# Reordering the opening of a fused attention and feed-forward kernel: pieces of W_v and three copies out of PSUM

## The chip, the cores and the metric

The kernel runs on one core of a Trainium2 chip. Its time is the device time of one execution in microseconds (us); the median of several executions is compared. The engines are TensorE (PE in the profile), VectorE (DVE), ScalarE (ACT), GpSimd (POOL) and SyncE (SP). Each works through its own queue in program order, and semaphores order them among each other. SP issues nearly all DMAs here.

## The reference

One transformer block on x, 2048 rows of width 640, in bf16: attention with a linear kernel, then a gated feed-forward network, each on a layer-normed input and with a residual.

```
h  = x + A(layernorm(x));   result = h + B(layernorm(h))
A: q, k, v = split(x @ wqkv)                      # 32 heads of width 20
   pq, pk = q @ w_phi, k @ w_phi                  # per head
   phi = concat(softmax(p), softmax(-p))          # for q and for k
   kv = phi_k^T v;  z = sum(phi_k)                # over the rows
   o = (phi_q kv) / (phi_q z + 1e-6);  A = o @ wo
B: (gelu(x @ w_gate) * (x @ w_up)) @ w_down       # hidden width 1536
```

## The kernel before

**Tiles.** The 2048 rows are 16 tiles of 128 rows, four tiles to a block. The width of 640 is five chunks of 128 (`NC = 5`). A weight lies in SBUF with its rows split into these five chunks, so "row chunk c" of W_v is what the c-th product of a sum over the width needs. A product of v (`pv`) for one tile is ten matmuls: five row chunks for each of two halves of 320 columns.

**Stages.** The opening computes v for the first four tiles, "folds" w_phi into W_k (`fold`, L231 to 258, five folds, one for each chunk), and begins k. Then a loop over the 16 tiles computes k, its exponentials (`E`), their normalisation (`sk`, `rs`, `E`) and the sums over the rows (`kvp`). After that come q, the attention's output and the feed-forward network, which are nearly all matmuls.

**From x to v.** A tile of x is loaded, VectorE takes its statistics (`bn_stats` twice and an aggregate, L120 and L124), rstd is computed, and the tile is normalised (`ln`, L155 on VectorE, L150 on ScalarE). Tiles 0 to 3 are then transposed on TensorE into PSUM and copied back to SBUF (`transpose_to`, L163 and L164), on ScalarE for tiles 0 and 1 and on VectorE for tiles 2 and 3. From tile 4 on a transposing DMA does this (L166). For tiles 2 and 3 rstd is two small ScalarE operations (L130 and L131), for tile 3 put in the queue by hand between the copies of v of tiles 0 and 1 (`root[0]()`). From tile 4 on rstd is two GpSimd operations (L138 and L139). The result of v is copied out of PSUM by ScalarE (`v_ev`, L315).

**What sets the order.** The order of the opening is written out by hand, and every engine's queue follows it. `v_part(t, *cs)` issues the matmuls of tile t for the row chunks named. `ln_st(t, between=f)` puts f between the two `bn_stats` of the tile. The copy of fold d is on ScalarE when d is in `KA` and on VectorE otherwise. A pool of four two-bank PSUM tiles (`psG0`) serves transposes, v, folds and k: a matmul that starts a new tile waits until the copy out of the tile that lay there before is done. On SP's queue lie, in this order, the loads of x tiles 0, 1 and 2, two loads of W_v, x tile 3, the third load of W_v, x tiles 4 and 5, five transposing loads of W_k, x tiles 6 and 7 (L469); and then, in turn, the transposing DMA of each normalised tile and further loads of x. A queue that waits for a tile to be normalised holds what stands behind it.

Of the kernel before, what the change touches and what calls it, by code (L numbers as in the profile page):

```python
# [17 lines left out]
def kernel(  # L18
# [12 lines left out]
    nc = tc.nc  # L31
    P = 128
    S = 2048
    D = 640
# [10 lines left out]
    H0 = [(P * c) // Dh for c in range(NC)]  # L45
    NH = [(P * c + P - 1) // Dh - H0[c] + 1 for c in range(NC)]
    VP = (0, 2, 4, 6, 7, 9, 11, 12)
    KA, QA = (0, 1, 4), (0, 1, 2, 3, 4)
    LQ = (7, 9, 9, 9, 10)
    FQ = (10, 11, 12, 13, 14)  # L50

# [22 lines left out]
    w_v = A_wqkv.rearrange("(c p) n -> p c n", p=P)  # L74
# [9 lines left out]
    x_sb = [const.tile([P, 4, D], BF16, name=f"x_sb{b}") for b in range(NB)]  # L84
# [22 lines left out]
    def small(pool, shape, name, bufs=3):  # L107
        return pool.tile(shape, F32, name=name, bufs=bufs)

    def gtile(name):  # L110
        return psG.tile([P, 2, 512], F32, name=name, tag="G")

    def ln_stats(pool, tiles, tag, act=True, between=None, log=False):

        n = len(tiles)
        mv = small(pool, [P, n, nc.vector.BN_AGGR_DIM], "mv" + tag)
        stats = small(pool, [P, n, 2, nc.vector.BN_STATS_DIM], "stats" + tag)
        for j, xt in enumerate(tiles):
            for i in range(2):
                nc.vector.bn_stats(stats[:, j, i, :], xt[:, i * HD:(i + 1) * HD])  # L120
                if between and i == j == 0:
                    between()
        for j in range(n):
            nc.vector.bn_aggr(mv[:, j, :], stats[:, j])  # L124
        ve = small(pool, [P, n], "ve" + tag)
        rstd = small(pool, [P, n], "rstd" + tag)
        if log is not False:

            def root():
                nc.scalar.activation(ve, mv[:, :, 1], ACTF.Ln, bias=eps)  # L130
                nc.scalar.activation(rstd, ve, ACTF.Exp, scale=-0.5)  # L131

            if log is True:
                root()
            else:
                log.append(root)
        else:
            nc.gpsimd.tensor_scalar_add(ve, mv[:, :, 1], EPS)  # L138
            nc.gpsimd.tensor_tensor(rstd, ve, nhalf[:, 0:n], op=ALU.pow)  # L139

        mr = small(pool, [P, n], "mr" + tag)
        if act:
            for j in range(n):
                nc.gpsimd.tensor_scalar(mr[:, j:j + 1], mv[:, j, 0:1], rstd[:, j:j + 1], -1.0,
                                        op0=ALU.mult, op1=ALU.mult)
        return [(xt, mv[:, j, 0:1], rstd[:, j:j + 1], mr[:, j:j + 1]) for j, xt in enumerate(tiles)]
# [11 lines left out]
    def transpose_to(dst, src, on_pe, on_dve=False):  # L158

        if on_pe:  # L160
            tp = psG.tile([P, 16, P], BF16, name="tp", tag="G")
            for c in range(NC):
                nc.tensor.transpose(tp[:, c, :], src[:, c * P:(c + 1) * P], ident)  # L163
            (nc.vector.tensor_copy if on_dve else nc.scalar.copy)(dst, tp[:, 0:NC, :])  # L164
        else:
            nc.sync.dma_start_transpose(dst, src)  # L166
# [7 lines left out]
    p1 = p1_cm.__enter__()  # L174
    Wv = p1.tile([P, NC, D], BF16, name="Wv")
# [14 lines left out]
    nc.scalar.dma_start(wphi, phi_v.rearrange("(c p) f -> p c f", p=P))  # L190
    nc.scalar.add_instruction(mybir.InstLoadActFuncSet(name=nc.get_next_instruction_name(), act_func_set_id=6))
    nc.sync.dma_start(x_sb[0][:, 2:3, :], x_v[:, 2:3, :])
    nc.sync.dma_start(Wv[:, 0:2, :], w_v[:, 0:2, 2 * D:3 * D])
    nc.sync.dma_start(Wv[:, 2:4, :], w_v[:, 2:4, 2 * D:3 * D])
    nc.sync.dma_start(x_sb[0][:, 3:4, :], x_v[:, 3:4, :])
    nc.sync.dma_start(Wv[:, 4:5, :], w_v[:, 4:5, 2 * D:3 * D])
    nc.sync.dma_start(x_sb[1][:, 0:2, :], x_v[:, 4:6, :])

    def load_T(WT, i, *ds):
# [25 lines left out]
    def warm(*cols):  # L225
        for n in cols:
            nc.tensor.matmul(wu[:, 0, 0:n], lhsT=ones[:, 0:P], rhs=ones[:, 0:n], start=True, stop=True)
# [3 lines left out]
    def fold(WT, W2, quarters, ds=range(NC)):  # L231


        n, w = (2, QF) if quarters else (1, HD)
        runs = []
        for c in range(NC):
            lo, hi = H0[c] * Dh, (H0[c] + NH[c]) * Dh
            for r in range(2 * n):
                a, b = max(lo, r * w), min(hi, (r + 1) * w)
                if a < b:  # L240
                    runs.append((r // n, r, c, a, b))
        runs.sort()
        for d in ds:
            wa = gtile("wa")
            wr = wa.rearrange("p u (q x) -> p (u q) x", q=n)
            for i, (u, r, c, a, b) in enumerate(runs):
                nc.tensor.matmul(wr[:, r, a - r * w:b - r * w], lhsT=WT[:, c, d * P:(d + 1) * P],  # L247
                                 rhs=BD[:, c].rearrange("p a b -> p (a b)")[:, a - H0[c] * Dh:b - H0[c] * Dh],
                                 start=(i == 0 or runs[i - 1][0] != u),
                                 stop=(i + 1 == len(runs) or runs[i + 1][0] != u), skip_group_check=True)  # L250
            dst, src = W2[:, d, :].rearrange("p (u f) -> p u f", u=2), wr[:, :, 0:w]
            if quarters:
                dst = W2[:, d, :].rearrange("p (c r f) -> p r c f", c=NC, r=4)
                src = src.rearrange("p r (c f) -> p r c f", c=NC)
            if d in (QA if quarters else KA):
                nc.scalar.copy(dst, src)
            else:
                nc.vector.tensor_copy(dst, src)
# [6 lines left out]
    def ln_0(t):  # L265
        xt, mean, rstd, mr = lnp[t] = ln_stats(p1, [x_sb[0][:, t, :]], f"c{t}", False, None, True)[0]
        nc.gpsimd.tensor_scalar(nrstd[t], rstd, -1.0, None, op0=ALU.mult)
        if t == 0:
            nc.gpsimd.tensor_scalar(mr, mean, nrstd[0], None, op0=ALU.mult)
        xc = fp.tile([P, D], BF16, name="xc", bufs=2)  # L270
        nc.vector.tensor_scalar(xc, xt, mean, None, op0=ALU.subtract)
        return xc

    def ln_st(*tiles, act=True, between=None, log=False):
        for t, v in zip(tiles, ln_stats(p1, [x_sb[t // 4][:, t % 4, :] for t in tiles], "1", act, between, log)):
            lnp[t] = v

    def ln_ap(t, on_act=False, on_pe=False):
        ln = (ln_act if on_act else ln_dve)(p1, "1", *lnp[t])
        if on_pe:  # L280
            lnp[t] = ln
        else:
            transpose_to(LN1T[t // 4][:, :, t % 4 * P:(t % 4 + 1) * P], ln, False)

    def ln_tp(t, on_dve=False):
        transpose_to(LN1T[t // 4][:, :, t % 4 * P:(t % 4 + 1) * P], lnp[t], True, on_dve)

    def lnT(t, c):
        b, tl = divmod(t, 4)
        return LN1T[b][:, c, tl * P:(tl + 1) * P]  # L290
# [14 lines left out]
    def v_part(t, *cs):  # L305

        if 0 in cs:
            pv[t] = gtile("pv")
        for c in cs:
            for u in range(2):  # L310
                nc.tensor.matmul(pv[t][:, u, 0:HD], lhsT=lnT(t, c), rhs=Wv[:, c, u * HD:(u + 1) * HD],
                                 start=(c == 0), stop=(c == NC - 1))

    def v_ev(t):
        nc.scalar.activation(vS[t % NV][:, :, 1:VC].rearrange("p (u h) f -> p u h f", u=2),  # L315
                             pv[t][:, :, 0:HD].rearrange("p u (h f) -> p u h f", f=Dh), ACTF.Copy,
                             scale=lnp[t][2] if t in CT else 1.0)
# [123 lines left out]
    tr_c(0)  # L441
    tr_c(1)
    ln_st(2, act=False, log=True)
    bd(0, NC)
    st_act(1, 1)
    warm(*[P] * 4)
    v_part(0, 0, 1)
    v_part(1, 0, 1)
    ln_ap(2, on_pe=True)
    v_part(0, 2, 3)  # L450
    root = []
    ln_st(3, act=False, between=lambda: ln_tp(2, True), log=root)
    v_part(0, 4)
    v_ev(0)
    v_part(1, 2, 3)
    root[0]()
    v_part(1, 4)
    v_ev(1)
    v_part(2, *range(NC))
    d = ident.rearrange("p (r j) -> p r j", r=4)  # L460
# [2 lines left out]
    for s, j in ((0, VC + 1), (1, 0)):  # L463
        nc.gpsimd.tensor_scalar(sc[:, s:s + 1], row[:, 0, j:j + 1], -1.0, 1.0, op0=ALU.mult, op1=ALU.add)
        nc.gpsimd.tensor_scalar(bi[:, s:s + 1], row[:, 0, VC:VC + 1], 0.5e-6, row[:, 0, j:j + 1],
                                op0=ALU.mult, op1=ALU.add)
    ln_st(4, act=False, between=lambda: ln_ap(3, on_pe=True))
    ln_tp(3, True)
    nc.sync.dma_start(x_sb[1][:, 2:4, :], x_v[:, 6:8, :])  # L469
    fold(WkT, Wk2, False, (0,))  # L470
    v_ev(2)
    fold(WkT, Wk2, False, (1,))
    ln_st(5, act=False, between=lambda: ln_ap(4))
    nc.sync.dma_start(x_sb[2][:, 0:2, :], x_v[:, 8:10, :])
# [18 lines left out]
    for t in range(NT):  # L493
        if t == T3:
            kvp = gtile("kvp")[:, 0, 0:2 * QF].rearrange("p (s f) -> p s f", s=2)
        late = t in (1, 4)
# [186 lines left out]
    def attn_ds(t, between=None):  # L683

        st[t] = ln_stats(p2, [x_sb[t // 4][:, t % 4, :]], "2", False, between)[0]
# [205 lines left out]
```

## Time and profile before

| | us |
|---|---|
| median of 3 runs | 273.07 (272.91 to 273.39) |
| the profiled execution | 272.66 |
| its span (first to last instruction) | 270.9 |
| TensorE busy | 267.0 (99%) |
| VectorE busy | 175.1 (65%) |
| ScalarE busy | 138.0 (51%) |
| GpSimd busy | 101.0 (37%) |
| TensorE share of the chain that ended last | 84% |
| VectorE share of it | 9% |

The page gives busy times over the whole span. The stages differ: in the stretch from 20 to 25 us VectorE is busy for 4.93 of 5.00 us, and from 229 us to the end for 12.88 of 41.9. TensorE's matmuls are pipelined and their ends modelled, so that its pauses are read from the starts of its instructions, group by group. The granted clock of TensorE is full in every slice of the profile. The chain that ended last is followed back from the last instruction; the stretches of the chain before 41 us are on SP, a DMA and VectorE, those after it on TensorE.

### The profile page before, as it was taken

What the parts mean: (1) busy time and instruction counts of PE and PEld (TensorE: products, weight loads), DVE (VectorE), ACT (ScalarE), POOL (GpSimd) and SP (SyncE); (2) the same over time, 40 slices, a digit from 0 to 9 for tenths busy, and PEclk for the clock granted to TensorE, in tenths of its full rate; (3) what the DMA queues carried; (4) which work ended last, traced back from release to release, by engine and by line L of the source; (5) the groups of instructions that cost most, each with busy time, mean ns of one, the idle gap of its engine ahead of it and who ended that gap; (6) DMA issues with size and microseconds to landing.
All of it is one profiled execution on the core that took longest, in us unless ns stands there. A gap on an engine that the chain in (4) does not pass through costs nothing.

```text
span 270.9 us, 7003 instructions
## 1 busy us (share of the span) xinstructions
PE 267.0 (99%) x2862; PEld 171.3 (63%) x2862; DVE 175.1 (65%) x333; ACT 138.0 (51%) x238; POOL 101.0 (37%) x231
## 2 busy tenths in 40 slices
PE   8999999999999999999999999999999999999995
PEld 7777777764455887788755555774555576444574
DVE  5899999998876756694467783347768432333322
ACT  5769996887789675345433356114345600332100
POOL 5448988794002336383222564003165400000000
PEclk9999999999999999999999999999999999999999
DMA  7987255441679433232301222110122311000011
GB/s 192 220 199 173 52 97 99 49 85 70 234 253 250 142 99 63 65 73 51 73 4 51 48 48 51 48 52 0 51 48 51 50 48 51 24 0 0 2 48 48
DMA packets 45263, 22.10 MB, mean 82 GB/s; under 512 B 37808, under 2 KB 43184, under 8 KB 45232
## 3 DMA queue, kind: packets, MB, share of 16 engines
q1 hardware_dynamic: 44576, 21.64, 32.2%
q8 instruction: 22, 0.36, 0.6%
q10 hardware_dynamic: 656, 0.03, 0.2%
q14 instruction: 9, 0.07, 0.1%
HBM read 10.18 MB, written 2.62 MB: 47 GB/s over the span
## 4 chain that ended last, share of the span: by engine, by line
PE 84%; DVE 9%; SPq 4%; DMA 2%; issue 1%; POOL 0%; DVEq 0%; POOLq 0%
PE gu L721 39%; PE pd L740 19%; PE pq L395 8%; PE po L661 8%; DVE sk L346 4%; PE pk L295 3%; DVE stats L120 3%; SPq L202 2%; PE ab L587 2%; PE pv L295 2%; DMA x_sb<-in_A_x_dram 2%; PE kvp L373 1%; DVE rs L350 1%; DVE E L354 1%; PE wa L247 1%
## 5 line engine op out<-in xcount | busy, mean ns | idle before, releaser
L724 ACT ACTIVATE g<-gu 128x512 bf16<-128x512 f32 (+1 forms) x60 | 30.6, 511 | 63.3 <-PE gu L721 62.4
L727 DVE TENSOR_TENSOR GT<-gu,g 128x512 bf16<-128x512 f32 (+1 forms) x60 | 34.3, 578 | 43.9 <-PE gu L721 31.1
L721 PE MATMUL gu<-LN2T,Wg 128*128 128x512 bf16 (+1 forms) x300 | 61.8, 337 | 0.0
L721 PE MATMUL gu<-LN2T,Wu 128*128 128x512 bf16 (+1 forms) x300 | 61.7, 336 | 0.0
L740 PE MATMUL pd<-Wd,GT 128*128 128x320 bf16 (+2 forms) x396 | 53.5, 295 | 0.0
L740 PEld LDWEIGHTS <-GT 128*128 128x128 bf16 x396 | 37.9, 98 | 14.6 <-DVE GT L727 0.2
L721 PEld LDWEIGHTS <-Wu 128*128 128x128 bf16 x300 | 29.4, 98 | 22.6
L721 PEld LDWEIGHTS <-Wg 128*128 128x128 bf16 x300 | 28.6, 98 | 20.3
L295 PEld LDWEIGHTS <-LN1T 128*128 128x128 bf16 x290 | 27.9, 98 | 10.6 <-issue 0.2
L743 DVE TENSOR_TENSOR y<-pd,x_sb 128x320 bf16<-128x320 f32 (+2 forms) x29 | 13.9, 480 | 29.5 <-PE pd L740 29.5
L354 POOL TENSOR_TENSOR E<-E,rs 128x640 bf16<-128x640 bf16 x24 | 30.3, 1290 | 6.5 <-DVE rs L350 2.6
L661 PE MATMUL po<-Wo,oT 128*128 128x320 bf16 x160 | 24.5, 299 | 0.0
L295 PE MATMUL pk<-Wk,LN1T 128*128 128x320 bf16 x160 | 24.4, 299 | 0.0
L395 PE MATMUL pq<-LN1T,Wq 128*128 128x512 bf16 x100 | 22.9, 379 | 0.0
L346 DVE TENSOR_REDUCE sk<-E 128x64 f32<-128x1280 bf16 x16 | 22.9, 1430 | 0.0
L400 ACT ACTIVATE Eq<-pq 128x1024 bf16<-128x1024 f32 (+1 forms) x26 | 19.9, 831 | 2.8 <-PE pq L395 2.7
L150 ACT ACTIVATE ln<-x_sb,v,rstd 128x640 bf16<-128x640 bf16 x14 | 12.9, 920 | 14.5 <-POOL v L700 14.4
L339 ACT ACTIVATE E<-pk 128x640 bf16<-128x640 f32 x28 | 18.8, 748 | 2.4 <-PE pk L295 1.8
L661 PEld LDWEIGHTS <-oT 128*128 128x128 bf16 x160 | 15.4, 98 | 6.9 <-ACT oT L164 0.2
L295 PE MATMUL pv<-Wv,LN1T 128*128 128x320 bf16 x130 | 19.8, 299 | 0.0
L636 DVE TENSOR_TENSOR tt<-AB,w 128x1280 bf16<-128x1280 f32 x12 | 17.8, 1485 | 1.0 <-POOL w L629 0.9
L616 POOL TENSOR_TENSOR pr<-AB 128x64 f32<-128x64 f32 x10 | 6.8, 678 | 26.7 <-DVE AB L597 20.6
(114 smaller groups left out, 291.2 us busy)
## 6 DMA issues: line engine op xcount, KB each, us to landing
out_dram<-y SPq DMA_DIRECT2D x15, 160.0 KB, 1.8
x_sb<-in_A_x_dram SPq DMA_DIRECT2D x6, 320.0 KB, 3.6
Wu<-in_B_w_up_dram SPq DMA_DIRECT2D x1, 1920.0 KB, 9.1
Wg<-in_B_w_gate_dram SPq DMA_DIRECT2D x2, 768.0 KB, 5.7
Wd<-in_B_w_down_dram SPq DMA_DIRECT2D x1, 1440.0 KB
Wo<-in_A_wo_dram SPq DMA_DIRECT2D x1, 800.0 KB, 4.8
x_sb<-in_A_x_dram SPq DMA_DIRECT2D x4, 160.0 KB, 3.3
Wv<-in_A_wqkv_dram SPq DMA_DIRECT2D x2, 320.0 KB, 4.2
```

The lines of the kernel that those rows point to most:

```text
L295: nc.tensor.matmul(ps[:, u, 0:HD], lhsT=lnT(t, c), rhs=W[:, c, u * HD:(u + 1) * HD], start=(c == 0), stop=(c == NC - 1))
L339: nc.scalar.activation(Ek[t][:, s, :].rearrange("p (u f) -> p u f", u=2), pk[:, :, 0:HD], ACTF.Exp, scale=((lnp[t][2], nrstd[t]) if t in C ...
L346: nc.vector.reduce_sum(sk, Ek[t].rearrange("p s (h f) -> p (s h) f", f=Dh), axis=AX.X)
L354: eng.tensor_tensor(e, e, rs[:, s * H:(s + 1) * H, None].to_broadcast([P, H, Dh]), ALU.mult)
L395: nc.tensor.matmul(pqs[j][:, i, :], lhsT=Wq2[:, kc, c * P:(c + 1) * P], rhs=LN1T[b][:, kc, :], start=(kc == 0), stop=(kc == NC - 1))
L400: nc.scalar.activation(Eq[j][:, :, s, :], pqs[j][:, 0:len(QG[j])], ACTF.Exp, scale=(1.0, -1.0)[s])
L636: nc.vector.tensor_tensor(tt.rearrange("p s (h f) -> p s h f", f=Dh), num, w[:, :, :, None].to_broadcast([P, 2, H, Dh]), ALU.mult)
L661: nc.tensor.matmul(pos[u], lhsT=st[t][:, c, :], rhs=Wo[:, c, u * HD:(u + 1) * HD], start=(c == 0), stop=(c == NC - 1))
L721: nc.tensor.matmul(gu[i][:, 0:n], lhsT=W[:, c, f * P:(f + 1) * P], rhs=LN2T[b][:, c, a0:a1], start=(c == 0), stop=(c == NC - 1))
L724: nc.scalar.activation(g[:, 0:n], gu[0][:, 0:n], ACTF.Gelu_apprx_tanh)
L727: nc.vector.tensor_tensor(st[b, "g", f][:, a0:a1], gu[1][:, 0:n], g[:, 0:n], ALU.mult)
L740: nc.tensor.matmul(ps, lhsT=st[b, "g", f][:, tl * P:(tl + 1) * P], rhs=Wd[:, f, f0:f1], start=(f == 0), stop=(f == NF - 1))
```

## The change

Six edits in the opening. Nothing is computed that was not computed before, and each engine's instructions are the same except for one copy.

1. The three loads of W_v carry one, two and two row chunks instead of two, two and one.
2. The products of v for tiles 0 and 1 follow these pieces: chunk 0 of both tiles, chunks 1 and 2 of both, then, after the transposes of tile 2, chunks 3 and 4 of both.
3. The transposes of tile 2 come after all products of chunks 0 to 2.
4. The copy of tile 3's transposes stands on VectorE's queue ahead of tile 4's aggregate, through the new argument `late` of `ln_stats`.
5. The copy of v tile 2 (`v_ev(2)`) stands on ScalarE's queue ahead of the copies of the folds.
6. The copy of the third fold (d = 2) is on ScalarE instead of VectorE.

```diff
-    KA, QA = (0, 1, 4), (0, 1, 2, 3, 4)
+    KA, QA = (0, 1, 2, 4), (0, 1, 2, 3, 4)
...
-    def ln_stats(pool, tiles, tag, act=True, between=None, log=False):
+    def ln_stats(pool, tiles, tag, act=True, between=None, log=False, late=None):
...
+        if late:
+            late()
         for j in range(n):
             nc.vector.bn_aggr(mv[:, j, :], stats[:, j])
...
-    nc.sync.dma_start(Wv[:, 0:2, :], w_v[:, 0:2, 2 * D:3 * D])
-    nc.sync.dma_start(Wv[:, 2:4, :], w_v[:, 2:4, 2 * D:3 * D])
+    nc.sync.dma_start(Wv[:, 0:1, :], w_v[:, 0:1, 2 * D:3 * D])
+    nc.sync.dma_start(Wv[:, 1:3, :], w_v[:, 1:3, 2 * D:3 * D])
     nc.sync.dma_start(x_sb[0][:, 3:4, :], x_v[:, 3:4, :])
-    nc.sync.dma_start(Wv[:, 4:5, :], w_v[:, 4:5, 2 * D:3 * D])
+    nc.sync.dma_start(Wv[:, 3:5, :], w_v[:, 3:5, 2 * D:3 * D])
...
-    v_part(0, 0, 1)
-    v_part(1, 0, 1)
+    v_part(0, 0)
+    v_part(1, 0)
     ln_ap(2, on_pe=True)
-    v_part(0, 2, 3)
+    v_part(0, 1, 2)
+    v_part(1, 1, 2)
     root = []
     ln_st(3, act=False, between=lambda: ln_tp(2, True), log=root)
-    v_part(0, 4)
+    v_part(0, 3, 4)
     v_ev(0)
-    v_part(1, 2, 3)
     root[0]()
-    v_part(1, 4)
+    v_part(1, 3, 4)
     v_ev(1)
     v_part(2, *range(NC))
...
-    ln_st(4, act=False, between=lambda: ln_ap(3, on_pe=True))
-    ln_tp(3, True)
+    ln_st(4, act=False, between=lambda: ln_ap(3, on_pe=True), late=lambda: ln_tp(3, True))
     nc.sync.dma_start(x_sb[1][:, 2:4, :], x_v[:, 6:8, :])
+    v_ev(2)
     fold(WkT, Wk2, False, (0,))
-    v_ev(2)
     fold(WkT, Wk2, False, (1,))
```

More of the change, by code (lines that the diff above doesn't have):

```diff
@@ L272, in ln_0, with ln_st @@
         return xc
-    def ln_st(*tiles, act=True, between=None, log=False):
-        for t, v in zip(tiles, ln_stats(p1, [x_sb[t // 4][:, t % 4, :] for t in tiles], "1", act, between, log)):
+    def ln_st(*tiles, act=True, between=None, log=False, late=None):
+        for t, v in zip(tiles, ln_stats(p1, [x_sb[t // 4][:, t % 4, :] for t in tiles], "1", act, between, log, late)):
             lnp[t] = v
```

## The prediction

> **What bounds the kernel now.** I read the page's busy shares and its chain of waits first:
>
> ```profile
> PE 267.0 (99%) x2862; PEld 171.3 (63%) x2862; DVE 175.1 (65%) x333; ACT 138.0 (51%) x238; POOL 101.0 (37%) x231
> ...
> PE 84%; DVE 9%; SPq 4%; DMA 2%; issue 1%; POOL 0%; DVEq 0%; POOLq 0%
> ```
>
> TensorE (PE) is 99% busy and carries 84% of the chain. Only its few pauses, or whatever makes it start late, can be worth time. The chain by time says where it is not TensorE (start, length, what):
>
> ```profile
> 11.48 4.08 DMA x_sb<-in_A_x_dram
> ...
> 15.59 0.90 DVE stats L120 x2
> ...
> 39.67 1.23 DVE E L354
> ...
> 40.94 0.38 PE kvp L373 x32
> ```
>
> Until 40.9 us the end hangs on VectorE (DVE): a load of x lands at 11.48 + 4.08 = 15.56, the row statistics of tile 6 start at 15.59, and from there VectorE runs without a pause until its product at 39.67 ends and releases TensorE at 40.94. ScalarE (ACT) runs back to back from 21.56 on, started there by the statistics of tiles 8 and 9. After 40.94 TensorE has no pause. So a shift of that first statistics instruction is a shift of the end, one for one; TensorE's own pauses before 40.9 count only if they exceed its slack. That slack is its pause at 40.94: the 128 small products around it run from 39.73 to 41.25, 1.52 us, where 64 of them take 0.63 (30.85 to 31.49), so about 0.26 us is pause. The timeline of the stretch that the change rewrites (start, length, engine, line, out<-in):
>
> ```profile
> 5.68 1.29 ACT L164 COPY LN1T<-tp 128x640 bf16<-128x640 bf16 x2 [0.37 <-PE tp L163]
> ...
> 6.45 1.90 PE L311 MATMUL pv<-Wv,LN1T 128*128 128x320 bf16 x12
> ...
> 8.19 0.44 PE L163 MATMUL tp<-ident,ln 128*128 128x128 bf16 x5
> ...
> 8.47 2.61 PE L311 MATMUL pv<-Wv,LN1T 128*128 128x320 bf16 x18
> ...
> 8.94 0.79 ACT L315 ACTIVATE vS<-pv,rstdc 128x640 bf16<-128x640 f32 x1 [0.73 <-PE pv L311]
> ...
> 10.16 0.20 ACT L131 ACTIVATE rstd<-ve 128x1 f32<-128x1 f32 x1
> ...
> 10.40 0.47 DVE L155 TENSOR_SCALAR ln<-x_sb,mv,rstd 128x640 bf16<-128x640 bf16 x1 [0.24 <-ACT rstd L131]
> ...
> 10.93 0.45 PE L163 MATMUL tp<-ident,ln 128*128 128x128 bf16 x5
> ...
> 11.21 1.22 PE L247 MATMUL wa<-BD,WkT 128*128 128x140 bf16 x18
> 11.30 0.21 DVE L124 BATCH_NORM_AGGREGATE mv<-stats 128x2 f32<-128x12 f32 x1
> 11.42 0.48 DVE L164 COPY LN1T<-tp 128x640 bf16<-128x640 bf16 x1
> ...
> 12.47 1.52 PE L295 MATMUL pv<-Wv,LN1T 128*128 128x320 bf16 x10
> ...
> 12.50 0.45 DVE L155 TENSOR_SCALAR ln<-x_sb,mv,rstd 128x640 bf16<-128x640 bf16 x1 [0.20 <-POOL rstd L139]
> ...
> 12.98 1.25 SPq L166 DMA_TRANSPOSE LN1T<-ln  x1
> ...
> 13.51 1.66 DVE L258 CAST Wk<-wa 128x640 bf16<-128x640 f32 x2
> ...
> 14.28 0.58 SPq L474 DMA_DIRECT2D x_sb<-in_A_x_dram  x1
> 15.09 0.43 DVE L155 TENSOR_SCALAR ln<-x_sb,mv,rstd 128x640 bf16<-128x640 bf16 x1
> ...
> 15.59 0.89 DVE L120 BATCH_NORM_STATS2 stats<-x_sb 128x6 f32<-128x320 bf16 x2
> ```
>
> Reading it: in "6.45 PE x12" the products of v follow each other at (8.19-6.45-0.1)/12 = 0.136 us, the 0.1 being lost at the first two; five transposes take 0.28 (8.19 to 8.47). The 18 fold matmuls from 11.21 would end after three times 0.31 us (a later group of six: 13.83 to 14.14), at 12.15, but the next product starts at 12.47. So TensorE loses 0.32 there: the third fold waits for the PSUM tile of tile 3's transposes (copy 11.42 to 11.90), the product after it for the first fold's copy on ScalarE (11.73 to 12.42). These are the pauses that the change touches.
>
> **The sum, step by step**, on the profiled execution: span 270.9, time 272.66, so 1.76 outside the span. The median of the runs is 273.07, 0.41 above; I add that at the end.
>
> *W_v in pieces 1, 2, 2.* Still three loads at the same places of SP's queue, each issued in 0.43 to 0.47 us, so nothing behind them moves, the fold weights' transposing loads and the x load of 11.48 included. By the issue rows the first piece lands at 2.18 + 4.2 = 6.4 and the last at 3.68 + 4.5 = 8.2, so 160 KB of the queue take about 0.45. The new first piece lands near 5.95. It releases nothing: the first product also waits for ScalarE's copy of tile 0, over at 5.68 + 0.69 = 6.37. Gain 0 to 0.03. The second piece (row chunks 1 and 2) lands near 6.85, bounded by 6.4 and by the x load behind it, 3.17 + 4.5 = 7.7; it is wanted at 7.30. I take 6.85, cost 0; at 7.7 it would cost 0.4. The third is due at 8.2 and wanted at 8.67.
>
> *The new order of v products.* Tile 1's first product is now the third instead of the fifth. It needs ScalarE's second copy, over at 5.68 + 1.29 = 6.97, and starts 0.06 later (10.87 to 10.93 for the same kind of wait), at 7.03 instead of 6.83. The ten products to the transposes of tile 2 take 1.36, so these start at 8.39 instead of 8.19: +0.20. After them come four products of tile 0 instead of two, so the copy of v tile 0 starts at 8.94 + 0.20 + 0.27 = 9.41 and frees ScalarE at 10.1. Queued behind it are the two small ScalarE operations on tile 3's statistics. VectorE has these at 10.01 (9.80 + 0.20), so ScalarE is now last: rstd is ready at 10.63 (10.36 before), the normalised tile 3 starts at 10.67 (10.40), its transposes at 11.19 (10.93): +0.26. TensorE would be free for them at 11.12, so at least +0.19 whatever ScalarE does; without the wait at 6.97 the shift would be near 0. I keep 0 to 0.4 for this term.
>
> *Tile 3's copy out of PSUM ahead of tile 4's aggregate.* Before, the aggregate (11.30) ran ahead of the copy (11.42). Now it queues behind it: the copy at 11.42 + 0.26 = 11.68 to 12.16, the aggregate at 12.08 to 12.29 instead of 11.30 to 11.51, +0.78. GpSimd (rstd) and VectorE's normalisation of tile 4 follow: 13.28 instead of 12.50. That holds VectorE's next statistics, so tile 5's aggregate ends at 14.38 instead of 13.60, and its rstd on GpSimd at 15.33 instead of 14.55. On SP's queue tile 4's transposing DMA goes out at 13.76 instead of 12.98, and the x load for tiles 8 and 9 behind it at 15.06 instead of 14.28.
>
> *The third fold's copy on ScalarE instead of VectorE.* VectorE loses one of the two copies in the row at 13.51 (0.83). Before, these were what tile 5's normalisation (15.09) waited for, with rstd ready 0.5 earlier. Now rstd is last: normalisation at 15.37 to 15.81 and statistics of tile 6 at 15.73 instead of 15.59. So the 0.83 taken away and the 0.78 of delay leave +0.28 at that normalisation, and +0.14 at the chain, since before it waited 0.14 for the landing at 15.56. On ScalarE the copy runs at 13.19 to 13.88 and is wanted at 14.64: hidden by 0.76.
>
> *v tile 2 copied before the folds.* The third fold now takes the PSUM tile of v tile 2 (ScalarE 11.32 to 12.02, so free at 12.08; TensorE arrives at 12.11), the product after it that of tile 3's transposes (12.16 plus 0.05, TensorE at 12.42). Both pauses go: TensorE is at 12.42 instead of 12.47, so it has made up the 0.26. Gain 0.05, which the chain does not use.
>
> *What stays covered.* Tile 4's transposed x would land at 13.76 + 3.2 = 16.9 (3.2 being its row's time to landing); its product comes at 17.13, after 17.18. Cover 0.2, and then TensorE's 0.26. The x load lands at 15.06 + 3.0 = 18.1; VectorE wants it at 18.14 + 0.14 = 18.28. Cover 0.2, and here nothing behind it.
>
> Sum: +0.14 us on the chain. 272.66 + 0.14 + 0.41 = **273.2 us**, no change that can be told. A measurement of this kernel tells about 0.2% (0.55 us) from no change; its three runs lie 0.48 apart.
>
> The clock: transposes take 0.107 us each at 4.93 and 0.056 at 8.19, while the pauses of 0.1 and 0.2 around 12 us are followed by products at the full 0.136. So the new pause of 0.2 at 6.83 should leave the rate alone. The Trainium skill, "TensorE: Matmul & The Clock Gate", "What's actually happening", says that the array goes from half to full rate after a busy window and back after an idle one, and that the window runs freely, so the switch point differs from run to run. By that rule 0.2 us is too short to fall back, and the trace agrees; no run here shows the window. If the switch came later in the new kernel, that is a rival below.
>
> **Rivals.**
> *No shift at all* (12%): ScalarE's copies or GpSimd come some 0.15 earlier, and the statistics still start at the landing, 15.56. Then 273.07.
> *Faster* (8%): the copy taken from VectorE counts. Against it: rstd of tile 5, and the landing at 15.56. If tile 3 is not late, tile 5's normalisation could start at 14.6, where rstd is ready, and the statistics at 14.96, a gain of 0.63, but only if the x load has landed by then, 0.6 earlier than in this execution. Then 272.4; below a landing at 15.04 it decides.
> *Slower by the x load for tiles 8 and 9* (17%): issued 0.78 later with 0.2 of cover. Its time to landing is 3.0 in its row, 4.1 for the load before it, 4.9 for the one at 4.16. At 4.1 it lands at 19.16, 0.88 late: 273.2 + 0.88 = 274.1. It decides from about 3.6 on (then +0.55 in all).
> *Slower by the clock* (3%): the half rate ran from 0.83 to about 6.6. If it lasts another 1.2 us, the products cost 0.6 more: 273.8; all the way to the first fold, 2.3 more, 275.5. By the skill's free window either kernel can meet this.
> *Late second piece of W_v* (4% beyond the bound): at 7.7, +0.4, so 273.6.
> The change does what it says: the built order of both kernels differs on each queue by just these moves.
>
> **How the numbers follow.** My forecast has 56%: 273.2, with 272.8 to 273.6 of its own from the 0 to 0.4 kept above. With the no-shift case and most of the late piece, "within 0.2%" (272.5 to 273.6) has 72%. Faster has 8%. Slower has 20%: x load 17, clock 3. The range goes down to 272.6 and up to 274.0, leaving the fastest case and the upper part of the late load out.
>
> **What would show it.** Right: the first products of v in a 2 + 2 pattern with a pause near 6.9; copy ahead of aggregate near 11.7; no gap before the product at 12.4; tile 5's normalisation ended last by GpSimd; the statistics of tile 6 at 15.7; the pause at 40.94 still ended by VectorE. Wrong: those statistics at 15.4 or earlier, a wait for x near 18.3, TensorE pausing at 17.1 for tile 4's transposed x, or 0.107 us per transpose at 8.4.

## The result and the profile after

The median went from 272.84 us (272.41 to 273.39) to 273.81 us (273.47 to 274.09): ratio 1.0032, 95% interval 1.0017 to 1.0046, or 0.5 to 1.3 us. These are eight executions of each kernel; the 273.07 us further up is the median of the first three of them. The change makes the kernel slower by 0.3%. The profiled execution has a span of 272.0 us, 1.1 more than before.

The page's busy shares and the shares of the chain of waits, after:

```profile
PE 266.0 (98%) x2843; PEld 170.9 (63%) x2862; DVE 174.3 (64%) x332; ACT 138.5 (51%) x239; POOL 100.7 (37%) x231
...
PE 92%; DMA 3%; DVE 2%; ACT 1%; issue 1%; POOL 1%; ACTq 0%
```

TensorE's 1.0 us less is not work saved: 19 of its matmul records are missing (2843 instead of 2862). What changed is the chain: VectorE held 9% of it before and holds 2% now. The stretch of the timeline that the change rewrites, after (start, length, engine, line, out<-in; most line numbers are two higher here than in the kernel before, and one higher further down):

```profile
7.04 1.53 PE L313 MATMUL pv<-Wv,LN1T 128*128 128x320 bf16 x10
...
8.41 0.44 PE L165 MATMUL tp<-ident,ln 128*128 128x128 bf16 x5
...
9.43 0.79 ACT L317 ACTIVATE vS<-pv,rstdc 128x640 bf16<-128x640 f32 x1 [1.21 <-PE pv L313]
...
11.68 0.49 DVE L166 COPY LN1T<-tp 128x640 bf16<-128x640 bf16 x1
...
12.09 0.20 DVE L126 BATCH_NORM_AGGREGATE mv<-stats 128x2 f32<-128x12 f32 x1
...
12.42 1.52 PE L297 MATMUL pv<-Wv,LN1T 128*128 128x320 bf16 x10
...
15.36 0.45 DVE L157 TENSOR_SCALAR ln<-x_sb,mv,rstd 128x640 bf16<-128x640 bf16 x1 [0.24 <-POOL rstd L141]
...
15.72 0.88 DVE L120 BATCH_NORM_STATS2 stats<-x_sb 128x6 f32<-128x320 bf16 x2
...
20.39 0.85 PE L297 MATMUL pv<-Wv,LN1T 128*128 128x320 bf16 x5 [0.39 <-DMA LN1T<-ln]
```

Nearly every step stands where it was forecast:

| us | before | forecast | after |
|---|---|---|---|
| third product of v | 6.83 | 7.03 | 7.04 |
| transposes of tile 2 | 8.19 | 8.39 | 8.41 |
| copy of v tile 0 | 8.94 | 9.41 | 9.43 |
| transposes of tile 3 | 10.93 | 11.19 | 11.18 |
| tile 4's aggregate | 11.30 | 12.08 | 12.09 |
| product of v tile 3 | 12.47 | 12.42 | 12.42 |
| tile 5's normalisation | 15.09 | 15.37 | 15.36 |
| statistics of tile 6 | 15.59 | 15.73 | 15.72 |
| x tiles 8 and 9 landed | 17.28 | 18.1 | 18.35 |
| statistics of tile 8 | 18.14 | 18.28 | 18.37 |
| TensorE: product of v for tile 5 | 19.89 | not named | 20.39 |

So the opening explains a third of the loss at most. VectorE's product at 39.8 ends at 41.12 instead of 40.88, 0.24 late, and TensorE a further 0.08: it waited at 20.39 for tile 5's transposed x, came to the products of 40 us 0.51 late instead of early, and found no pause left there to absorb it (41.57 instead of 41.25 after them, +0.32):

```profile
39.82 1.30 DVE L356 TENSOR_TENSOR E<-E,rs 128x640 bf16<-128x640 bf16 x1
...
40.23 1.41 PE L375 MATMUL kvp<-E,vS 128*32 128x40 bf16 x128
...
41.57 1.53 PE L297 MATMUL pv<-Wv,LN1T 128*128 128x320 bf16 x10
```

The rest is far from the change. The waits of TensorE between 125 and 135 us, after (engine, line, waited for: us in all, times, longest):

```profile
PE pd L741 <- DVE GT L728: 0.6, 1, 0.6
```

Between 41 and 125 us TensorE keeps its +0.32 to +0.36; after this one wait it is +1.12 to the end. The same place in the timelines, first before, then after:

```profile
129.47 0.76 ACT L724 ACTIVATE g<-gu 128x256 bf16<-128x256 f32 x2
129.58 3.42 PE L740 MATMUL pd<-Wd,GT 128*128 128x320 bf16 x24
...
129.87 0.81 DVE L727 TENSOR_TENSOR GT<-gu,g 128x256 bf16<-128x256 f32 x2 [1.37 <-ACT g L724]
```

```profile
129.83 0.76 ACT L725 ACTIVATE g<-gu 128x256 bf16<-128x256 f32 x2
...
130.23 0.81 DVE L728 TENSOR_TENSOR GT<-gu,g 128x256 bf16<-128x256 f32 x2 [1.37 <-ACT g L725]
130.71 2.47 PE L741 MATMUL pd<-Wd,GT 128*128 128x320 bf16 x17 [0.60 <-DVE GT L728]
```

The two lines on VectorE are its products for hidden chunks 10 and 11. ScalarE and VectorE run alike in both, 0.36 us later in the second. But before, the first product of the down projection (`pd`) starts while VectorE is still at work. After, it waits until the first of VectorE's two products is over (130.65) and starts 0.05 later. The last matmul ahead of it started at 129.83 and takes 0.11, so the pause is 130.71 - 129.94 = 0.77 us. And 0.24 + 0.08 + 0.77 = 1.09, the whole of the 1.1.

Why should `pd` wait for chunk 10 in one kernel only? It reads that chunk's result only 1.4 us later. What it needs at its start is a place in PSUM, and the built kernels list which place each tile was given. Up to this point PSUM is four places of two banks (0, 2, 4, 6). At the marked point `split` (a stage of the second block of gate and up, just ahead of these products) they become eight single banks, and `pd` takes bank 0 in both kernels. The last users of the four places:

| tile | before | after | before_places_2 | before_places_6 |
|---|---|---|---|---|
| gate and up, chunk 7 | 2 | 0 | 0 | 4 |
| gate and up, chunk 8 | 4 | 2 | 2 | 0 |
| output product of tile 7 | 0 | 4 | 4 | 2 |
| gate and up, chunk 9 | 6 | 6 | 6 | 6 |
| gate and up, chunk 10 | 2 | **0** | **0** | 4 |
| gate and up, chunk 11 | 4 | 2 | 2 | **0** |
| first `pd` after the split | 0 | 0 | 0 | 0 |

Before, bank 0 had belonged to tile 7's output product, which VectorE read at 126.6. After, it belongs to chunk 10. The difference begins in the opening: with edit 5 the third fold gets place 4 (that of v tile 2) instead of 0, the product behind it 0 instead of 2, the next fold 2 instead of 4, and every later tile up to the split follows the same exchange, 0 for 2, 2 for 4, 4 for 0. While the places rotate this is a mere renaming. At the split, where bank numbers are fixed, it is not. (The last two columns belong to experiments.)

### The profile page after: what moved, and what is told of

Same layout as the page of the kernel before. It is cut to its first block, busy times and chain, and to the rows that moved or that the text cites. A ratio compares the mean times of both kernels' runs of the same rounds, so it can differ in the third digit from the quotient of the medians.

```text
span 272.0 us, 6984 instructions
## 1 busy us (share of the span) xinstructions
PE 266.0 (98%) x2843; PEld 170.9 (63%) x2862; DVE 174.3 (64%) x332; ACT 138.5 (51%) x239; POOL 100.7 (37%) x231
## 4 chain that ended last, share of the span: by engine, by line
PE 92%; DMA 3%; DVE 2%; ACT 1%; issue 1%; POOL 1%; ACTq 0%
PE gu L722 38%; PE pd L741 19%; PE po L662 8%; PE pq L397 8%; PE pk L297 7%; PE pv L297 6%; PE ab L588 2%; PE kvp L375 2%; DMA LN1T<-ln 2%; PE pv L313 1%; DMA x_sb<-in_A_x_dram 1%; PE tp L165 1%; PE wa L249 1%; ACT LN1T L166 0%; POOL rstd L141 0%
## 5 line engine op out<-in xcount | busy, mean ns | idle before, releaser
L722 PE MATMUL gu<-LN2T,Wg 128*128 128x512 bf16 (+1 forms) x287 | 61.1, 335 | 0.7
```

The lines of the kernel that those rows point to most:

```text
L722: nc.tensor.matmul(gu[i][:, 0:n], lhsT=W[:, c, f * P:(f + 1) * P], rhs=LN2T[b][:, c, a0:a1], start=(c == 0), stop=(c == NC - 1))
```

## The experiments

Two theories of the pause near 130 us. **A, places:** edit 5 renames the PSUM places, and `pd` meets one that is in use. **B, phase:** everything arrives some 0.3 us later, and the pause comes from that.

**Edits apart: all but edit 5, and edit 5 alone.** In the first, the copy of v tile 2 stays where it was:

```diff
-    v_ev(2)
     fold(WkT, Wk2, False, (0,))
+    v_ev(2)
     fold(WkT, Wk2, False, (1,))
```

> Edits 1, 2, 3, 4 and 6 are made, the copy of v tile 2 (edit 5) stays behind the first fold's copy. Theory A (places in PSUM): edit 5 alone changes which PSUM tile each later user gets; from the split of PSUM into single banks on, the first product of the down projection (near 130.7 us) then lies where gate and up of hidden chunk 10 were, and waits 0.77 us for VectorE. Without edit 5 there is no pause there, and what is left is the opening: 0.2 to 0.35 us slower than before. Theory B (phase): the pause at 130.7 us comes because everything arrives 0.3 us later than before; the opening is as late here as in the changed kernel, so the pause is there too: 1.0 to 1.1 us slower than before.

Measured: ratio 1.0005 (0.9996 to 1.0014), 273.22 against 272.97 us; no pause near 130. The second is the kernel before with the same lines the other way round.

> Only the copy of v tile 2 moves ahead of the first fold's copy. Theory A (places in PSUM): the opening is as before, and the first product of the down projection near 130.4 us waits 0.7 to 0.8 us for VectorE's product of hidden chunk 10: 0.75 us slower than before. Theory B (phase): nothing is late, so no pause near 130: within 0.1 us of before.

Measured: ratio 1.0034 (1.0022 to 1.0047), 273.94 against 272.97 us, with a pause of 0.77 us in the predicted place. Its timeline there:

```profile
130.38 0.81 DVE L727 TENSOR_TENSOR GT<-gu,g 128x256 bf16<-128x256 f32 x2 [1.37 <-ACT g L724]
...
130.85 0.84 PE L740 MATMUL pd<-Wd,GT 128*128 128x320 bf16 x5 [0.60 <-DVE GT L727]
```

One edit of six carries the loss, and it is the one that had been costed at a gain of 0.05. B is not quite out yet: in this execution x landed 0.5 us later than in that of before, so the kernel was late here too.

**The split two products later, in both kernels.** The idea was to let the two down products keep a two-bank place that is free.

```diff
-          attn_at(7, 0, SHORT) + [(12, split), (14, attn_one, 8), (17, attn_one, 9), (18, attn_one, 10), (20, attn_one, 11)] + attn_rest(8, 15) +
+          attn_at(7, 0, SHORT) + [(14, split), (14, attn_one, 8), (17, attn_one, 9), (18, attn_one, 10), (20, attn_one, 11)] + attn_rest(8, 15) +
```

> All six edits, and the split of PSUM into eight single banks comes two products of the down projection later, so that those two still take a two-bank tile that has long been free. Theory A (places in PSUM): the pause of 0.77 us at 130.7 us is gone, and 0.2 to 0.35 us slower than before is left. Theory B (phase): the pause stays in that place or moves on by a product, as VectorE is as late as it was: 1.0 to 1.1 us slower than before.

> The kernel before, with the split of PSUM two products later, as a control for the run with all six edits. Both theories: no pause near 130 us in either, so within 0.1 us of before. If it is faster than that, the later split is worth something by itself, and the run with all six edits has to be read against this one.

Measured: 1.0059 (1.0046 to 1.0073) with all edits, and 1.0030 (1.0018 to 1.0041) for the control that was to change nothing. Both expectations missed. The pause at the first `pd` is gone in both, but the move makes one of the same kind. From the control's timeline (`ab` is the attention's product of tile 8, `y` the copy of `pd`):

```profile
133.18 0.82 DVE L746 TENSOR_TENSOR y<-pd,x_sb 128x640 bf16<-128x640 f32 x1 [2.36 <-PE pd L740]
134.06 0.47 PE L587 MATMUL ab<-KV,Eq 32*128 32x44 bf16 x40 [0.92 <-DVE y L746]
```

The first bank after the later split is part of the place that `pd` itself still holds (with all six edits it is the fourth); TensorE waits 1.08 us for VectorE's copy of it, and 0.96 us with all six edits. Which places the split meets matters in either kernel; this move only chose other bad ones. (With all six edits the median is 0.9 us worse than the control's, though both profiled spans are 272.0. 0.2 to 0.35 of it was expected. About 0.4 lies outside the span, between an execution's time and the span of its instructions: 2.04 to 2.12 us in each of the six executions, where the control has 1.68 to 1.74. What that time is stays open.) A way to change the places without changing the work was needed.

**Other places, the same work.** The code has such a handle: for one tile the two halves of the attention's PSUM pair are copied out in swapped order, which swaps two places from there on.

```diff
-        for u in ((1, 0) if t in (4,) else (0, 1)):
+        for u in ((1, 0) if t in (6,) else (0, 1)):
```

With tile 6 instead of 4, the six edits get the places of before at the end:

> All six edits, and the two halves of one PSUM pair are copied out in swapped order for tile 6 instead of tile 4 (the same two ScalarE copies, 70 to 110 us into the run). That gives every tile from hidden chunk 7 of the second block of gate and up on the place that it has in the kernel before: the first product of the down projection at 130 us then takes a place that has been free since the output product of tile 7. Theory A (places): no pause there; 0 to 0.35 us slower than before, the opening alone. Theory B (phase): the pause stays, since nothing arrives earlier: 1.0 us slower.

Measured: ratio 1.0010 (1.0001 to 1.0019), 273.29 against 273.05 us. No pause; its timeline:

```profile
130.28 1.52 PE L741 MATMUL pd<-Wd,GT 128*128 128x320 bf16 x10
...
130.57 0.81 DVE L728 TENSOR_TENSOR GT<-gu,g 128x256 bf16<-128x256 f32 x2 [1.37 <-ACT g L725]
```

Here everything arrives later than in the profile of the changed kernel (VectorE's two products at 130.57 instead of 130.23), and `pd` does not wait. That speaks against B. The reverse, on the kernel before, with its opening untouched, tile 2 and tile 6 in the handle:

> The kernel before, with the swapped order for tile 2 instead of tile 4: its opening is untouched, and the places from hidden chunk 7 on become those of the changed kernel. Theory A (places): a pause of 0.77 us ahead of the first product of the down projection near 130.4 us, and 0.77 us slower than before. Theory B (phase): no pause, within 0.1 us of before.

> The kernel before, with the swapped order for tile 6 instead of tile 4: now the first product of the down projection lies where hidden chunk 11 was, whose product on VectorE ended at 130.68 in the profile of before. Theory A (places): it starts at 130.74 instead of 129.58, a pause of 1.15 us, and 1.15 us slower than before. Theory B (phase): no pause, within 0.1 us of before.

Measured: 1.0032 (1.0020 to 1.0045) and 1.0043 (1.0029 to 1.0057). The timelines of the two, tile 2 first:

```profile
130.01 0.81 DVE L727 TENSOR_TENSOR GT<-gu,g 128x256 bf16<-128x256 f32 x2 [1.37 <-ACT g L724]
130.49 1.38 PE L740 MATMUL pd<-Wd,GT 128*128 128x320 bf16 x9 [0.61 <-DVE GT L727]
```

```profile
130.11 0.81 DVE L727 TENSOR_TENSOR GT<-gu,g 128x256 bf16<-128x256 f32 x2 [1.37 <-ACT g L724]
130.98 0.84 PE L740 MATMUL pd<-Wd,GT 128*128 128x320 bf16 x5 [0.99 <-DVE GT L727]
```

The pauses are 0.77 and 1.15 us by the starts, as theory A gave them to the hundredth: the first waits for chunk 10, the second for chunk 11. The unchanged opening with the changed kernel's places costs as much as the whole change (1.0032 both). Theory B has fallen.

**The opening, piece by piece.** What is left after the places is 0.24 us (0.03 to 0.52). Three runs take it apart:

The kernel before with edits 1, 2 and 3:

```diff
-    nc.sync.dma_start(Wv[:, 0:2, :], w_v[:, 0:2, 2 * D:3 * D])
+    nc.sync.dma_start(Wv[:, 0:1, :], w_v[:, 0:1, 2 * D:3 * D])
...
-    v_part(0, 0, 1)
-    v_part(1, 0, 1)
+    v_part(0, 0)
+    v_part(1, 0)
...
```

The changed kernel without edit 4, with the handle at tile 6:

```diff
-    ln_st(4, act=False, between=lambda: ln_ap(3, on_pe=True), late=lambda: ln_tp(3, True))
+    ln_st(4, act=False, between=lambda: ln_ap(3, on_pe=True))
+    ln_tp(3, True)
```

The kernel before with edits 5 and 6, with the handle at tile 6:

```diff
-    KA, QA = (0, 1, 4), (0, 1, 2, 3, 4)
+    KA, QA = (0, 1, 2, 4), (0, 1, 2, 3, 4)
...
+    v_ev(2)
     fold(WkT, Wk2, False, (0,))
-    v_ev(2)
```

> Only the pieces of W_v and the order of the products of v; places in PSUM as before. By the sum: tile 3's transposes come 0.2 to 0.3 us later, tile 4's aggregate still runs ahead of tile 3's copy, both fold copies stay on VectorE, and tile 5's normalisation, which follows them, moves by at most 0.26 us; the statistics of tile 6 at 15.6 to 15.8 us, 0 to 0.25 us slower than before. If the first products gain from the earlier first piece (0.25 us in the profile of the run without edit 5): 0.

> Edits 1, 2, 3, 5 and 6 with the places of before (swapped order for tile 6); tile 3's copy stays behind tile 4's aggregate. By the sum, edit 4 delays tile 4's aggregate by 0.5 of its 0.78 us and with it the load for x tiles 8 and 9: without it that load is issued at 14.3 to 14.6 and tile 5's normalisation no longer waits for GpSimd past 15.1, so the statistics of tile 6 start when x lands: 0 to 0.1 us slower than before, against 0.24 us with edit 4. Rival: the 0.24 us of the run with all edits and the places of before is the scatter of that x load and not edit 4; then this run is as slow, 0.2 to 0.3 us.

> Edits 5 and 6 with the places of before (swapped order for tile 6). One copy fewer on VectorE at 13.5 us and no pauses of TensorE around 12 us (0.43 us together), tile 3 not late. If x tiles 6 and 7 bind (landing 15.5 to 15.8 in most profiles): within 0.1 us of before. If VectorE's copies did: up to 0.5 us faster.

Measured: edits 1 to 3 alone 1.0015 (1.0005 to 1.0025); without edit 4 1.0023 (1.0010 to 1.0036); edits 5 and 6 alone 0.9988 (0.9977 to 0.9998), 272.84 against 273.02 us. So edit 4, which looked costliest on paper, is not shown to cost anything: leaving it out made nothing faster, and the expectation missed (0.3 to 1.0 us slower where 0 to 0.1 was expected, with the rival's 0.2 to 0.3 at the lower end). The pieces of W_v and the new order of v cost 0.1 to 0.7 us.

Edits 5 and 6, once the places are put right, gain 0.05 to 0.6 us: the only version faster than both kernels, by a margin that its interval barely separates from none. Of the 0.18 us between those two medians, some 0.08 lies outside the span (a median of 1.72 us against 1.80). The pauses around 12 us, 0.43 us in its expectation, are the 0.32 of the prediction by the starts.

The parts do not simply add up: edits 1 to 3 (+0.4) and edits 5 and 6 (-0.3) would give +0.1 together, and the run with both, the one without edit 4, gave +0.6; the intervals are wide enough to allow that. Which wait each of these goes through is open. The profiles can't say, since the opening differs more from execution to execution than from kernel to kernel, as the last section shows; the profiled execution without edit 4 was even the fastest of its twelve (272.61, median 273.43).

**Two attempts at the load of x tiles 6 and 7**, which nearly always starts VectorE's chain. First, on top of edits 5 and 6 with the places of before, this load ahead of the last two transposing loads of W_k:

```diff
-    load_T(WkT, 1, *range(NC))
+    load_T(WkT, 1, 0, 1, 2)
+    nc.sync.dma_start(x_sb[1][:, 2:4, :], x_v[:, 6:8, :])
+    load_T(WkT, 1, 3, 4)
```

> A version meant to be faster than both: edits 5 and 6 with the places of before (swapped order for tile 6), and the load of x tiles 6 and 7 moved ahead of the last two transposing loads of W_k. The statistics of tile 6 waited for that load (15.56) in the profile of before. If the load lands by 15.0, VectorE can start them once tile 5's normalisation is done, near 15.0, 0.55 us earlier, and TensorE loses the 0.43 us of pauses around 12 us: 0.4 to 0.6 us faster than before. If the two transposing loads that are pushed back, or some later load, hold the chain: within 0.2 us of before or slower.

Measured: 1.0031 (1.0020 to 1.0042). x landed at 12.75 instead of 15.56, but the fourth transposing load at 15.25 instead of 12.5, and the fourth fold waited for it:

```profile
15.29 0.49 PE L249 MATMUL wa<-BD,WkT 128*128 128x140 bf16 x6 [1.51 <-DMA WkT<-in_A_wqkv_dram]
...
15.82 0.82 DVE L260 CAST Wk<-wa 128x640 bf16<-128x640 f32 x1 [2.16 <-PE wa L249]
16.56 0.43 DVE L155 TENSOR_SCALAR ln<-x_sb,mv,rstd 128x640 bf16<-128x640 bf16 x1
```

VectorE held that fold's copy ahead of tile 5's normalisation, so the chain started 1.3 us late. A load issued 0.8 us later (9.64 instead of 8.84) landed 2.7 us later. (Here `pd` starts at 131.06, the latest of all runs, and without a pause: the places were those of before. Theory B would have it there.) Second, the load cut in two, one for each tile:

```diff
-    nc.sync.dma_start(x_sb[1][:, 2:4, :], x_v[:, 6:8, :])
+    nc.sync.dma_start(x_sb[1][:, 2:3, :], x_v[:, 6:7, :])
+    nc.sync.dma_start(x_sb[1][:, 3:4, :], x_v[:, 7:8, :])
```

> Edits 5 and 6 with the places of before, as in the run before, and the load of x tiles 6 and 7 as two loads, one per tile. In the profiles so far VectorE's product near 41 us ended 25.32 us after the landing of that load (within 0.06 us, in 11 of 13), and the last of its 16 engines came 0.1 to 1.5 us after the rest. If tile 6's half lands at 15.2 or earlier, tile 6's statistics start near 15.2, after tile 5's normalisation (14.75 to 15.2), instead of 15.6 to 15.8; TensorE's pause of 0.3 to 0.4 us near 41 goes first: 0.4 to 0.6 us faster than before, and 0.1 to 0.3 us faster than edits 5 and 6 with the places of before. Rival: the late engine holds both halves, or the second half 0.45 us later, so that tile 7's statistics wait instead: no faster than edits 5 and 6 with the places of before (0.33 us faster than before).

Measured: 1.0025 (1.0016 to 1.0034). The statistics of tile 6 did start earlier, but the next load took their place:

```profile
15.14 0.88 DVE L120 BATCH_NORM_STATS2 stats<-x_sb 128x6 f32<-128x320 bf16 x2
...
18.26 1.67 DVE L120 BATCH_NORM_STATS2 stats<-x_sb 128x6 f32<-128x320 bf16 x4 [0.49 <-DMA x_sb<-in_A_x_dram]
```

Tile 8's statistics waited for x tiles 8 and 9, and the lead of some 0.5 us was gone at 18.26. Neither sentence of the expectation named that. That makes it no faster; it does not make it slower. Against the executions of before that were timed beside it, it lost 0.7 us, where edits 5 and 6 with one load had gained 0.3. Some 0.3 us of that lies outside the span (2.05 to 2.14 us in each execution, 1.75 to 1.85 in those of before); the rest is not explained.

## Why the prediction was right and wrong

*Right: the opening.* The pause of 0.2 us for ScalarE's copy, the 0.26 at tile 3, the aggregate at 12.08, GpSimd as the one that ends last before tile 5's normalisation, the 0.14 at tile 6's statistics: all within 0.03 us of the profile. The pieces of W_v landed at 5.91 and 6.73 (forecast 5.95 and 6.85) and kept nothing waiting, so the rival of the late second piece is out. The clock held: transposes at 8.41 follow each other at 0.056 us, as before. But the half rate did end at another time, as that rival allowed: near 5.9 us here and 6.7 before, and between 4.1 and 6.7 over the fourteen profiles of this case. (The page's clock row is full all the same; the rate shows in the starts of the matmuls, 0.107 or 0.056 us apart.) In three profiles with the new pieces of W_v in which it ended early, ScalarE's first copy was over at 6.14 to 6.16, and the first product started at 6.20 to 6.22 instead of 6.45, a gain that the prediction had put at 0 to 0.03. With the places put back, the six edits cost 0.27 us by the ratio (0.03 to 0.52), and the five without edit 5 cost 0.14 (-0.11 to 0.38); the forecast of 0.14 lies in both intervals.

*Mis-sized: the load for x tiles 8 and 9.* Forecast to land at 18.1 with 0.2 of cover; it was issued at 15.01 as forecast, but took 3.34 us instead of 3.0, landed at 18.35 and cost VectorE 0.10 (0.23 late at tile 8's statistics, 0.13 at tile 6's). That is the rival's mechanism at a tenth of its price, and the wait for x near 18.3 that the prediction had listed as a sign of being wrong.

*The rival "faster":* with edits 5 and 6 alone and the places of before, the copy taken from VectorE does bring tile 5's normalisation to 14.75, and the kernel is faster by 0.05 to 0.6 us, on the scale of the 0.6 that this rival promised. Its profile does not show the gain, though: the statistics of tile 6 waited there for x, which landed at 15.75, as the rival's own condition has it. In the changed kernel edit 4 and the order of v put that normalisation at 15.36.

*Missed: tile 5's transposing DMA.* "What stays covered" named that of tile 4 and not this one. From the chain of waits, after:

```profile
15.83 4.52 DMA LN1T<-ln
20.39 1.53 PE pv L297 x10
```

Issued 0.28 later, it took 4.52 us to land, where before it took 2.67 (15.55 to 18.22). That ate the 1.7 us between 18.22 and its product at 19.89, and TensorE's whole slack at 41 us, so the pause there that VectorE was to end, a sign of being right in the prediction, is gone. In the end it cost 0.08 beyond VectorE's delay, because that slack was there. The two profiles are extremes: over all fourteen this DMA took 2.40 to 4.52 us, and 3.37 in the one with all six edits and the places of before. The 0.08 belongs to this execution, and is not shown to be a cost of the change.

*Wrong: where the likeliest case stopped.* The forecast, +0.14 us and no change that can be told, failed (measured 0.5 to 1.3 us slower), and it failed at two statements. "After 40.94 TensorE has no pause. So a shift of that first statistics instruction is a shift of the end, one for one" held for the kernel before and was carried over to another one. And "the built order of both kernels differs on each queue by just these moves" is true and not enough: the order of instructions was compared, the places of their tiles were not. The paragraph on the copy of v tile 2 saw the exchange begin ("The third fold now takes the PSUM tile of v tile 2 (...), the product after it that of tile 3's transposes (...)"), booked the two pauses that it removes, and did not follow the rotation to where it ends. The term is missing from the sum: 0.77 us, against 0.14 for all the rest. That the measured time lies inside the range is luck: the range reached up to 274.0 for another reason, the x load.

The Trainium skill, "Perfetto Trace Analysis", "Matmuls", says that independent groups of matmuls should rotate through different PSUM banks, so that copying one out overlaps the next group. The runs agree and sharpen it: at 130 us the banks do rotate, and it is the age of the bank that decides, free since 127.4 (before, no pause), in use until 130.65 (the changed kernel, 0.77 us) or until 130.92 (tile 6 in the handle of before, 1.15 us).

## What to carry to other kernels

When an edit changes the order in which buffers come free, compare which buffer each later tile gets, down to the end of the pool and past any point where the pool is cut anew; the instruction order alone does not show it. A new wait far behind the edit, for an engine that has not slowed down, is the sign. It can be tested without touching the work, by changing the order of two releases, and put right the same way: edit 5 alone cost 0.34%, and edits 5 and 6 with the places of before came out 0.12% faster (0.02% to 0.23%).

## What the runs showed of the hardware

The start of VectorE's chain wanders by itself. SP's five transposing loads of W_k, ahead of the load for x tiles 6 and 7, in the timelines of the changed kernel and of the six edits with other places:

```profile
4.64 6.64 SPq L204 DMA_TRANSPOSE WkT<-in_A_wqkv_dram  x5
11.32 0.58 SPq L470 DMA_DIRECT2D x_sb<-in_A_x_dram  x1
```

```profile
4.64 7.44 SPq L204 DMA_TRANSPOSE WkT<-in_A_wqkv_dram  x5
12.12 0.58 SPq L470 DMA_DIRECT2D x_sb<-in_A_x_dram  x1
```

Both issue the same loads in the same order. Four of the five take 1.26 to 1.31 us each in all fourteen profiles, but for one of 1.22 in the run that puts a load of x among them; the third took 1.33 to 2.15. From the chain of waits of the second:

```profile
7.29 2.15 SPq L204
...
12.12 4.12 DMA x_sb<-in_A_x_dram
```

Apart from the two attempts at that load, the load behind them then took 4.0 to 4.4 us to land, between 15.52 and 16.24, and VectorE's product near 41 us ended 25.31 to 25.38 us after that landing in 11 of 14 profiles (25.52 in the changed kernel, where GpSimd and the load of x tiles 8 and 9 held the chain; the other two are the attempts). In the two kernels above, whose openings are the same, it landed at 15.60 and 16.24. So 0.6 to 0.7 us of the opening is scatter that one profiled execution hides, as much as any of the edits there was measured to be worth. What lengthens the third issue, and whether the pieces of W_v do, stays open: with the new pieces it took 1.33, 1.39, 1.48, 1.49, 1.86 and 2.15, with the old ones 1.41 to 1.69.
